# Twenty-two identity transposes at the start, and a QKV tile between two sets of transposes, in an attention and GLU kernel

## The chip, the cores and the metric

The kernel runs on one core of a Trainium2 chip. The metric is the device time of one execution in microseconds (us): 1578.9 us is the median of three runs (1578.4 to 1580.97). The engines carry the profile's names: PE (matrix multiplies and transposes; PEld is its weight load), DVE, ACT, POOL, and SP, which here only issues DMAs. Each engine works through its own instructions strictly in the order in which they were put in its queue, and waits where one of them needs something that isn't there yet.

## The reference

One transformer block over 2048 tokens of width 576, in float32:

```python
x = A_x
h = x + _A_ref(_layernorm(x), A_wqkv, A_wo)      # 32 heads of 18, window 8, dilation 2
h2 = h + _B_ref(_layernorm(h), B_w_gate, B_w_up, B_w_down)   # (sigmoid(x Wg) * (x Wu)) Wd, 4608 wide
```

In the attention a token at position s sees only positions s, s-2, ..., s-14, so its parity and its half of the sequence split the tokens into four blocks of 512.

## The kernel before

**Tiles.** The tokens are four blocks (`BLOCKS`), each of four 128-token tiles j = 0 to 3. To keep float32 precision each operand of a multiply is split in two: a "hi" part, an ACT copy with rounding (L104 and its like, in `split`), and a "lo" part, a DVE subtraction (L105). The width of 576 is 512 + 64: the four main chunks have a hi and a lo tile (`th`, `tl`), the last 64 columns are held twice in a fifth chunk of `th`, whose lower half is made lo by DVE (L109, in `split_rest`). A product (`tok_major`) is 14 matmuls over these chunks; the last two (L159, L160) use the fifth chunk.

**The opening.** `opening()` loads the tokens of block 0 and the QKV weights of head group 0 (`wr`), and does block 0's layer norm, its transposes and its first four QKV tiles. Its order on each engine is written by hand: `ch(key, fn)` queues an instruction behind the last one of the same engine in this chain. Per tile j the chain has `stats` (DVE bn_stats, POOL power), `norm` (DVE L491, L492), `tr` (PE, four main transposes L497 into a bank of the tag `mm`, one of the rest, L499, into a bank of the tag `acc`), `x_hi` (ACT L504, L505), `x_lo` (DVE L509, L511), and `heads_of` (PE, one QKV tile). The weights have `w_hi(c)` (ACT L516) and `w_lo(c)` (DVE L519) for five chunks c. Behind it, `qkv_w(1, ...)` loads and splits the weights of head group 1 (`ws`, three buffers for five chunks; hi at L104, lo at L105). On DVE its lo parts are told to come after `x_lo(1)`; its hi parts on ACT are not part of the chain.

**What sets the order elsewhere.** A list scheduler orders each engine's instructions by priority (`tc.high_priority`), by explicit "after this one" marks (`tc.issue_after`) and by its own estimate of when operands are ready. An instruction that it believes ready early can so be put ahead of another of higher priority. The order is fixed when the kernel is built.

**QKV and attention.** The rest of the first 220 us are QKV tiles on PE (16 tiles for each head group) while the attention (`attention`, in steps between `yield`s) runs on DVE from stores of q, k and v in DRAM that are loaded again by SP. Its large steps are the products L189 and L215 and the reduction L193, some 2.5 us each.

**The front.** `front()` projects block 0's attention output with `wo`, adds the residual, and does the second layer norm and its transposes. It is a generator over four `proj_j`, one for each j, in lock step: the first `next(fr)` issues the main transposes of all four tiles (L146) and their splits, the second the rest transposes (L150) and their splits, the third and fourth the two halves of the projection (L157 and on, DVE L262), later ones the norm (L123 to L128) and its transposes. Every transpose set takes a PSUM bank in turn, of the `mm` tag (three) or the `acc` tag (five, shared with the QKV tiles). The first `next(fr)` waits for L226, the end of block 0's attention; the rest transposes wait for the L428 copies as well. Before the front, `more` has issued two QKV tiles of block 2; two more, and the four of block 3, are left to fill PE between the front's steps.

**After it** the GLU products begin (`single`, L746 and L753, with DVE L766 and ACT L793), with the attention of block 1 still going on DVE. When block 1's last group is done (L226), POOL stores it (L228, L230), SP loads it again (`oj`, L707), and `proj_scr` transposes it on PE.

Of the kernel before, what the change touches and what calls it, by code (L numbers as in the profile page):

```python
# [21 lines left out]
P = 128  # L22
# [38 lines left out]
def kernel(ctx, tc, x, wqkv, wo, wmlp, out):  # L61
    nc = tc.nc
    dve, act, pool, pe, sp = nc.vector, nc.scalar, nc.gpsimd, nc.tensor, nc.sync
# [14 lines left out]
    ident = cst.tile([P, P], F32, name="ident")  # L78
# [19 lines left out]
    def f32(ap):  # L98
        return ap.bitcast(F32)
# [30 lines left out]
    def ln_stats(xj, junk):  # L130
        mv = sm.tile([P, 2], F32, bufs=4, name="mv")
        rstd = sm.tile([P, 1], F32, bufs=4, name="rstd")
        act.activation(junk[:, :D], xj, AF.Copy, scale=-1.0 / D, accum_out=mv[:, 0:1])
        sq = act.activation(junk[:, :D], xj, AF.Square, bias=mv[:, 0:1], accum_out=mv[:, 1:2])
        pool.tensor_scalar(rstd, mv[:, 1:2], 1.0 / D, EPS, ALU.mult, ALU.add)
        pool.tensor_tensor(rstd, rstd, mhalf, ALU.pow)
        pool.tensor_tensor(mv[:, 0:1], mv[:, 0:1], rstd, ALU.mult)
        return mv[:, 0:1], rstd, sq
# [98 lines left out]
    def drain(gen):  # L237
        for _ in gen:
            pass
# [54 lines left out]
    def th_tile():  # L294
        return xt.tile([P, 5, TB], F32R, tag="th", bufs=3, name="th")

    def tl_tile():
        return xt.tile([P, 4, TB], F32R, tag="tl", bufs=4, name="tl")
# [24 lines left out]
    def mm_tile():  # L323
        return psp.tile([P, 512], F32, tag="mm", bufs=3, name="mm")

    def acc_tile():
        return psp.tile([P, 512], F32, tag="acc", bufs=5, name="acc")

    def tok_tile(shape=(P, NS, DX)):
        return stk.tile(list(shape), F32, tag="tok", bufs=2, name="tok")  # L330
# [7 lines left out]
    def load_x(b, js=range(NS), t=None):  # L338
        e, hf = BLOCKS[b]
        if t is None:  # L340
            t = sah.tile([P, NS, D], F32, bufs=2, name="h")
        for j in js:
            sp.dma_start(t[:, j], xv[e, hf][:, j])
        return t
# [26 lines left out]
    def raw_w(g):  # L371
        if g == 3:
            wr = sah.tile([P, NS, D], F32, bufs=2, name="h").rearrange("p j d -> p (j d)")
            wr = wr[:, :QC].rearrange("p (c n) -> p c n", c=5)
        else:
            wr = swo.tile([P, 5, NQ], F32, tag="wo", name="wr")
        for c in range(5):
            sp.dma_start(wr[:, c], wqkv[g][:, c * NQ:(c + 1) * NQ])
        return wr
# [16 lines left out]
    def qkv(b, g, T, w):  # L396
        e, hf = BLOCKS[b]
        ev = ev_tile([P, 3, NS, CG])
        for j in range(NS):
            ps = acc_tile()  # L400
            passes.append(tok_major(ps, NQ, *T, slice(j * P, (j + 1) * P), w[:, 0], w[:, 1]))
            with tc.high_priority(HI):
                act.activation(ev[:, :, j], ps[:, :NQ].rearrange("p (t c) -> p t c", t=3), AF.Copy)
            yield
        r0 = LP + hf * TB
        with tc.high_priority(HI):
            act.dma_start(qscr[b][g], ev[:, 0].rearrange("p j c -> p (j c)"))
            for t, s in ((1, kscr), (2, vscr)):
                act.dma_start(s[e][g][r0:r0 + TB, :].rearrange("(p j) c -> p (j c)", p=P),
                              ev[:, t].rearrange("p j c -> p (j c)"))  # L410
        emitted.add((b, g))
# [46 lines left out]
    def opening():  # L458
        xb = load_x(0, (0, 1))
        wr = raw_w(0)  # L460
        load_x(0, (2, 3), xb)
        th, tl = th_tile(), tl_tile()
        xn = tok_tile()
        qw = saw.tile([P, 2, 5, NQ], F32R, tag="qw", bufs=2, name="qw")
        T.append((th, tl))
        w.append(qw)
        last = {}

        def ch(key, fn):
            with ExitStack() as way:  # L470
                way.enter_context(tc.high_priority(3 * HI))
                if key in last:
                    way.enter_context(tc.issue_after(getattr(last[key], "ins", last[key])))
                last[key] = fn()

        nr, pv, pr = {}, {}, {}

        def stats(j):
            bs = sm.tile([P, 2, 6], F32, bufs=4, name="bs")
            mv = sm.tile([P, 2], F32, bufs=4, name="mv")  # L480
            rstd = sm.tile([P, 1], F32, bufs=4, name="rstd")
            nr[j] = mv[:, 0:1], rstd
            for k in range(2):
                ch(dve, lambda: dve.bn_stats(bs[:, k], xb[:, j, k * DH2:(k + 1) * DH2]))
            ch(dve, lambda: dve.bn_aggr(mv, bs))
            ch(dve, lambda: dve.tensor_scalar(rstd, mv[:, 1:2], EPS, None, ALU.add))
            ch(pool, lambda: pool.tensor_tensor(rstd, rstd, mhalf, ALU.pow))

        def norm(j):
            m, r = nr[j]  # L490
            ch(dve, lambda: dve.tensor_scalar(xn[:, j, :D], xb[:, j], m, r, ALU.subtract, ALU.mult))  # L491
            ch(dve, lambda: dve.tensor_copy(xn[:, j, D:DX], xn[:, j, DM:D]))  # L492

        def tr(j):
            pv[j], pr[j] = mm_tile(), acc_tile()
            for c in range(4):
                ch(pe, lambda: pe.transpose(pv[j][:, c * P:(c + 1) * P],  # L497
                                            xn[:, j, c * P:(c + 1) * P], ident))
            ch(pe, lambda: pe.transpose(pr[j][:, :P], xn[:, j, DM:DX], ident))  # L499

        def x_hi(j):
            js = slice(j * P, (j + 1) * P)
            pv[j] = pv[j].rearrange("p (c n) -> p c n", c=4)
            ch(act, lambda: act.activation(th[:, 0:4, js], pv[j], AF.Copy))  # L504
            ch(act, lambda: act.activation(th[:, 4, js], pr[j][:, :P], AF.Copy))  # L505

        def x_lo(j):
            js = slice(j * P, (j + 1) * P)
            ch(dve, lambda: dve.tensor_tensor(tl[:, :, js], pv[j], f32(th[:, 0:4, js]),  # L509
                                              ALU.subtract))  # L510
            ch(dve, lambda: dve.tensor_tensor(th[64:128, 4, js], pr[j][64:128, :P],  # L511
                                              f32(th[64:128, 4, js]), ALU.subtract))
            ends.append(last[dve])

        def w_hi(c):
            ch(act, lambda: act.activation(qw[:, 0, c], wr[:, c], AF.Copy))  # L516

        def w_lo(c):
            ch(dve, lambda: dve.tensor_tensor(qw[:, 1, c], wr[:, c], f32(qw[:, 0, c]),  # L519
                                              ALU.subtract))  # L520

        call = qkv(0, 0, T[0], qw)
        ends = []

        def heads_of(j):
            ch(pe, lambda: (next(call), passes[-1])[1])

        stats(0)
        stats(1)
        norm(0)  # L530
        w_hi(0)
        tr(0)
        norm(1)
        w_hi(1)
        tr(1)
        w_lo(0)
        w_hi(2)
        w_lo(1)
        x_hi(0)
        x_lo(0)  # L540
        w_hi(3)
        w_lo(2)
        w_hi(4)
        stats(2)
        x_hi(1)
        w_lo(3)
        w_lo(4)
        heads_of(0)
        with tc.high_priority(3 * HI):
            n3, r3, sq = ln_stats(xb[:, 3], xn[:, 3])  # L550
        norm(2)
        tr(2)
        x_lo(1)
        heads_of(1)
        x_hi(2)
        ch(act, lambda: act.activation(xn[:, 3, :D], xb[:, 3], AF.Identity, bias=n3, scale=r3))
        ch(act, lambda: act.activation(xn[:, 3, D:DX], xn[:, 3, DM:D], AF.Copy))
        x_lo(2)
        tr(3)
        heads_of(2)  # L560
        x_hi(3)
        x_lo(3)
        heads_of(3)
        drain(call)
        return ends
# [75 lines left out]
    fr = front()  # L641
# [10 lines left out]
        step(ag, 1)  # L652
    last = passes[-1]
    with tc.issue_after(getattr(last, "ins", last)):
        for _ in range(2):
            next(fr)
    for b in (2, 3):
        for j, _ in enumerate(more if b == 2 else qkv(b, 3, T[b], w[3])):
            with ExitStack() as way:
                if (b, j) == (2, 0):  # L660
                    way.enter_context(tc.issue_after(getattr(passes[-1], "ins", passes[-1])))
                next(fr, END)
            step(ag, 1)
        if b == 2:
            with tc.high_priority(2 * HI):
                wg = xt.tile([P, WC], F32, tag="tl", bufs=4, name="wg0")
                sp.dma_start(wg, wmlp[0])
                ww = first_split(wg)
# [699 lines left out]
```

## Time and profile before

| | before |
|---|---|
| median of 3 runs | 1578.9 us |
| profiled execution | 1584.01 us |
| its span, first to last instruction | 1582.2 us |
| PE busy | 1551.0 us (98%) |
| DVE busy | 1255.2 us (79%) |
| ACT busy | 879.2 us (56%) |
| POOL busy | 199.9 us (13%) |
| PE idle before its first work | 6.6 us |

The profiled execution was 1.8 us longer than its span, and 5.1 us longer than the median of the runs. PE is busy nearly throughout, and DVE in most of the first third (its 40 slices of the span read 9 from the sixth to the nineteenth). Times in the views are from the span's start.

### The profile page before, as it was taken

How to read it: one execution, taken by the hardware profiler on the slowest of the kernel's cores; microseconds unless marked ns; L12 is line 12 of the kernel's file. 1: busy time of each engine (PE TensorE's matmuls, PEld its weight loads, DVE VectorE, ACT ScalarE, POOL GpSimd, SP SyncE). 2: the span in 40 equal slices, each digit the busy share in tenths (PEclk: the TensorE clock that was granted, in tenths of full speed). 3: DMA queues.
4: the chain of work that ended last, by engine and by line, in shares of the span. 5: the costliest groups of instructions: out<-in, count | busy, mean ns of one | idle time of the engine just before them, and what ended most of it. 6: DMA issues, size and time to landing. Idle time of an engine off the chain costs nothing.

```text
span 1582.2 us, 22347 instructions
## 1 busy us (share of the span) xinstructions
PE 1551.0 (98%) x8520; PEld 1377.3 (87%) x8520; DVE 1255.2 (79%) x1883; ACT 879.2 (56%) x1584; POOL 199.9 (13%) x249
## 2 busy tenths in 40 slices
PE   8999999999999999999999999999999999999998
PEld 7999888887888888888888888888888888888887
DVE  6998999969999999999426588866777776677755
ACT  6632244435555645566542355766777766777660
POOL 2300000020000010000101010112112112111210
PEclk9999999999999999999999999999999999999999
DMA  8646445365566677664683524999899989999983
GB/s 284 215 168 220 179 185 190 108 235 183 133 167 170 164 176 192 157 162 109 161 242 125 181 81 126 193 181 177 170 180 186 173 173 181 173 173 186 181 169 120
DMA packets 77147, 273.95 MB, mean 173 GB/s; under 512 B 8336, under 2 KB 14224, under 8 KB 76144
## 3 DMA queue, kind: packets, MB, share of 16 engines
q0 software_dynamic: 28192, 107.29, 37.5%
q1 hardware_dynamic: 41216, 145.11, 27.2%
q10 hardware_dynamic: 7632, 20.12, 3.3%
q8 instruction: 66, 1.08, 0.3%
q14 instruction: 41, 0.34, 0.1%
HBM read 143.98 MB, written 130.87 MB: 174 GB/s over the span
## 4 chain that ended last, share of the span: by engine, by line
PE 58%; issue 16%; DVE 11%; DMA 8%; POOL 4%; ACT 2%; SPq 0%; ACTq 0%; POOLq 0%; DVEq 0%
PE b L746 27%; PE dp L864 13%; PE dp L926 6%; PE b L753 5%; PE acc L157 4%; POOL h L935 3%; DMA wg<-in_wmlp_dram 3%; DVE pr L189 2%; DVE pr L215 1%; DVE lg L193 1%; DVE w L105 1%; DVE pr L221 1%; PE b L157 1%; PE bgp L157 1%; DMA x<-tok 1%
## 5 line engine op out<-in xcount | busy, mean ns | idle before, releaser
L746 PE MATMUL b<-tl,w 128*128 128x512 f32 x1704 | 432.6, 393 | 5.1 <-ACT s L820 3.2
L746 PEld LDWEIGHTS b<-tl,w 128*128 128x128 f32 x1704 | 307.9, 188 | 63.6 <-ACT s L820 4.7
L746 PE MATMUL b<-th,w 128*128 128x512 f32 x1344 | 346.2, 392 | 1.5 <-DVE s L839 1.5
L746 PEld LDWEIGHTS b<-th,w 128*128 128x128 f32 x1344 | 244.8, 188 | 46.5 <-DVE s L839 1.9
L932 ACT ACTIVATE ev<-dp 128x576 f32<-128x576 f32 x224 | 144.7, 646 | 63.2 <-PE dp L926 58.9
L753 PE MATMUL b<-th,w 128*128 128x512 f32 x568 | 175.7, 390 | 0.0
L104 ACT ACTIVATE w<-wg 128x384 fp32r<-128x384 f32 (+1 forms) x186 | 110.8, 601 | 111.1 <-PE b L753 48.8
L935 POOL DMA_DIRECT2D h<-ev x128 | 110.0, 860 | 458.6 <-ACT ev L932 444.7
L157 PE MATMUL acc<-qw,th 128*128 128x432 f32 x512 | 154.3, 362 | 2.5 <-DVE th L109 2.3
L105 DVE TENSOR_TENSOR w<-wg,w 128x640 fp32r<-128x640 f32 (+1 forms) x186 | 120.8, 656 | 41.3 <-ACT w L104 41.1
L105 DVE TENSOR_TENSOR w<-tw,w 128x512 fp32r<-128x512 f32 x120 | 82.6, 688 | 82.1 <-ACT w L104 81.5
L753 PEld LDWEIGHTS b<-th,w 128*128 128x128 f32 x568 | 106.5, 188 | 23.2
L864 PE MATMUL dp<-d,h1h 128*128 128x288 f32 x640 | 119.9, 297 | 0.0
L864 PE MATMUL dp<-d,h0h 128*128 128x288 f32 x608 | 114.1, 297 | 0.8 <-DVE tail L874 0.8
L872 ACT ACTIVATE stage<-dp 128x576 f32<-128x576 f32 x104 | 66.9, 645 | 70.1 <-PE dp L864 69.8
L157 PEld LDWEIGHTS acc<-qw,th 128*128 128x128 f32 x512 | 96.6, 189 | 8.4 <-DVE th L109 3.5
L864 PEld LDWEIGHTS dp<-d,h1h 128*128 128x128 f32 x640 | 99.7, 190 | 3.0
L104 ACT ACTIVATE w<-tw 128x512 fp32r<-128x512 f32 x120 | 75.4, 628 | 46.5 <-PE b L746 40.0
L864 PEld LDWEIGHTS dp<-d,h0h 128*128 128x128 f32 x608 | 95.1, 190 | 4.3 <-DVE tail L874 1.0
L157 PE MATMUL acc<-qw,tl 128*128 128x432 f32 x256 | 92.6, 362 | 0.1
L189 DVE TENSOR_TENSOR pr<-kw,q 128x2304 f32<-128x2304 f32 x32 | 81.8, 2556 | 8.8 <-DMA kw<-k 8.7
L880 POOL DMA_DIRECT2D h<-stage x26 | 31.0, 1194 | 436.3 <-ACT stage L872 350.1
(310 smaller groups left out, 2955.5 us busy)
## 6 DMA issues: line engine op xcount, KB each, us to landing
h<-ev POOLq DMA_DIRECT2D x96, 576.0 KB, 7.1
wg<-in_wmlp_dram SPq DMA_DIRECT2D x47, 928.0 KB, 5.9
h<-stage POOLq DMA_DIRECT2D x26, 1152.0 KB, 9.5
wg<-in_wmlp_dram SPq DMA_DIRECT2D x36, 640.0 KB, 4.3
kw<-k SPq DMA_DIRECT2D x16, 792.0 KB, 5.2
vw<-v SPq DMA_DIRECT2D x16, 792.0 KB, 4.3
wd<-in_wmlp_dram SPq DMA_DIRECT2D x18, 576.0 KB, 7.4
h<-ev POOLq DMA_DIRECT2D x32, 288.0 KB, 6.9
```

Of the source, the lines that this page charges most:

```text
L104: act.activation(hi, src, AF.Copy)
L105: splits.append(dve.tensor_tensor(lo, src, f32(hi), ALU.subtract))
L157: pe.matmul(ps[:, :n], a[:, c, js], m[:, c], start=k == 0, stop=False)
L189: dve.tensor_tensor(pr, both(kw, u), q[:, us].unsqueeze(2).broadcast_to([P, 2, W, CG]), ALU.mult)
L746: pe.matmul(ps, wt[:, a, k0 + c], xx[:, m + c], start=first and k == 0, stop=k == 5, skip_group_check=True)
L753: pe.matmul(ps, wt[:, a, k0], xx[:, 4], start=False, stop=a == 1, skip_group_check=True)
L864: pe.matmul(ps[:, i, :DH2], a[:, js], d[:, m, i * DH2:(i + 1) * DH2], start=k == 0, stop=k == n)
L872: act.activation(hv, ps, AF.Copy)
L880: pool.dma_start(hacc[b], hs, accum_op=ALU.add, max_dma_last_dim=8 * D)
L926: pe.matmul(ps[:, i, :DH2], a[x][:, js], m[y], start=k in (0, 1, 3) and q == 0, stop=q == 2, skip_group_check=True)
L932: act.activation(hs[:, k % 2], ps[:, :, :DH2], AF.Copy)
L935: pool.dma_start(hsev[:, u, k0:k + 1], hs[:, :k + 1 - k0], accum_op=ALU.add, max_dma_last_dim=8 * D)
```

## The change

Two edits. In the opening, ahead of all other work on PE, 22 transposes of the identity into a bank of the tag `mm` that nobody reads. And in the front, the second `next(fr)`, which issues the rest transposes, moves from before the third QKV tile of block 2 to behind it.

```diff
         nr, pv, pr = {}, {}, {}
+        pre = mm_tile()
+        for _ in range(22):
+            ch(pe, lambda: pe.transpose(pre[:, :P], ident, ident))
...
     last = passes[-1]
     with tc.issue_after(getattr(last, "ins", last)):
-        for _ in range(2):
-            next(fr)
+        next(fr)
     for b in (2, 3):
         for j, _ in enumerate(more if b == 2 else qkv(b, 3, T[b], w[3])):
             with ExitStack() as way:
                 if (b, j) == (2, 0):
                     way.enter_context(tc.issue_after(getattr(passes[-1], "ins", passes[-1])))
+                    next(fr)
                 next(fr, END)
             step(ag, 1)
```

In the changed file the lines of the opening and the front stand three lower than before (L504 is L507, L516 is L519); L104, L105, L109, L146, L150, L157, L189, L193 and L262 keep their numbers. The diff alone doesn't show that the scheduler, which counts the 22 transposes as time in which ACT is free, puts other instructions elsewhere.

ACT in the opening, before. The rows are the engine, line, operation, output<-inputs, shape and count; `qw<-wr` is head group 0's weights, `qw<-ws` head group 1's, `th<-mm` and `th<-acc` the hi parts of the tokens:

```order
L516 ACTIVATE qw<-wr 128x432 x3
L504 ACTIVATE th<-mm 128x4x128
L505 ACTIVATE th<-acc 128x128
L516 ACTIVATE qw<-wr 128x432 x2
L504 ACTIVATE th<-mm 128x4x128
L505 ACTIVATE th<-acc 128x128
L104 ACTIVATE qw<-ws 128x432 x2
L133 ACTIVATE tok,mv<-h 128x576
L104 ACTIVATE qw<-ws 128x432
```

and with the change:

```order
L519 ACTIVATE qw<-wr 128x432 x3
L104 ACTIVATE qw<-ws 128x432 x3
L507 ACTIVATE th<-mm 128x4x128
L508 ACTIVATE th<-acc 128x128
L519 ACTIVATE qw<-wr 128x432 x2
L507 ACTIVATE th<-mm 128x4x128
L508 ACTIVATE th<-acc 128x128
L133 ACTIVATE tok,mv<-h 128x576
```

Three weight chunks of head group 1, each of which waits for its own load, now stand ahead of the hi parts of block 0's first tile. DVE's order in the opening is the same in both.

DVE in the front, before, from the reduction of block 1's attention that runs when the transposes are done (`tl<-...` are lo parts of the main chunks, `th<-...` of the rest, `pr<-kw,q` the attention's product, `h<-h,mm` the first projected tile):

```order
L193 TENSOR_REDUCE lg<-pr 128x128
L105 TENSOR_TENSOR tl<-mm,th 128x4x128
L109 TENSOR_TENSOR th<-acc,th 64x128 x3
L109 TENSOR_TENSOR th<-mm,th 64x128
L105 TENSOR_TENSOR tl<-mm,th 128x4x128
L105 TENSOR_TENSOR tl<-acc,th 128x4x128 x2
L189 TENSOR_TENSOR pr<-kw,q 128x2304
L262 TENSOR_TENSOR h<-h,mm 128x288
```

and with the change:

```order
L193 TENSOR_REDUCE lg<-pr 128x128
L105 TENSOR_TENSOR tl<-mm,th 128x4x128 x2
L105 TENSOR_TENSOR tl<-acc,th 128x4x128 x2
L189 TENSOR_TENSOR pr<-kw,q 128x2304
L109 TENSOR_TENSOR th<-acc,th 64x128 x3
L109 TENSOR_TENSOR th<-mm,th 64x128
L262 TENSOR_TENSOR h<-h,mm 128x288
```

The four rest parts moved from ahead of the attention's product to behind it.

PE at the same place, before (`acc<-qw,th` opens the QKV tile):

```order
L146 MATMUL mm<-ident,tok 128x128 x5
L150 MATMUL mm<-ident,tok 128x128
L146 MATMUL mm<-ident,tok 128x128 x3
L146 MATMUL acc<-ident,tok 128x128 x5
L150 MATMUL acc<-ident,tok 128x128 x3
L146 MATMUL acc<-ident,tok 128x128 x3
L157 MATMUL acc<-qw,th 128x432
```

and with the change:

```order
L146 MATMUL mm<-ident,tok 128x128 x8
L146 MATMUL acc<-ident,tok 128x128 x8
L157 MATMUL acc<-qw,th 128x432
...
L160 MATMUL acc<-qw,th 128x432
L150 MATMUL acc<-ident,tok 128x128 x3
L150 MATMUL mm<-ident,tok 128x128
```

The sixteen main transposes now come in one run, then the whole QKV tile, then the four rest transposes; before, the QKV tile came last. From there to about L864's first products DVE, ACT and PE also take the projection's tail and the norms in another order (the first two tiles' norms earlier, the last two later); behind that the three engines' orders are the same again.

## The prediction

> **What bounds the kernel now.** I read the page's first lines, then who waited for whom on PE over the whole span, then on PE between 13 and 179 us alone, then the chain of waits, and last the timelines of the two places that the change touches. The page:
>
> ```profile
> span 1582.2 us, 22347 instructions
> PE 1551.0 (98%) x8520; PEld 1377.3 (87%) x8520; DVE 1255.2 (79%) x1883; ACT 879.2 (56%) x1584; POOL 199.9 (13%) x249
> ```
>
> PE's waits over the span (line, releaser: us in total, times, longest), and after the "..." those between 13 and 179 us, where there is one:
>
> ```profile
> PE mm L497 <- DVE tok L491: 6.6, 1, 6.6
> PE b L146 <- DMA oj<-o: 4.2, 1, 4.2
> PE acc L157 <- DVE th L109: 2.3, 2, 1.6
> ...
> PE acc L157 <- DVE th L109: 0.6, 1, 0.6
> ```
>
> So PE has almost no slack from the opening to 179 us: what delays its start there arrives whole at 179 us. The change touches the time after the 6.6 us, and two stalls in the front, the 1.6 us above and one of 1.7 us. Whether these are worth anything is told by the chain of waits (start, us, what), here around 119 and 308 us:
>
> ```profile
> 119.17 0.54 ACT ev L403
> ...
> 128.47 2.57 DVE pr L189
> ...
> 307.86 0.68 DVE kw L226
> ...
> 309.46 6.85 DMA o<-kw
> ```
>
> ```profile
> 319.42 1.11 PE L146 MATMUL b<-ident,oj 128*128 128x128 f32 x4 [4.23 <-DMA oj<-o]
> ```
>
> Up to 119.17 the chain is PE; there the last q, k, v of a head group leave, DVE waits for them until 128.47, and from then to 308.54 it is the attention on DVE that counts. Its last result is stored and loaded, and PE stands for 4.23 us until 319.42. **Two consequences.** A delay of PE in the opening goes through 119 us into DVE's chain and out at 319 us. And PE time saved in the front, at 180 to 190 us, is not saved at 319 us: it makes the 4.23 us longer, unless DVE's own chain gets shorter there.
>
> **The opening: ACT's order.** Before, ACT, DVE, SP and PE did this (start, us, what), with the landing of the third `ws` load in the last line (us from its issue):
>
> ```profile
> 7.75 0.60 ACT L504 ACTIVATE th<-mm 128x512 fp32r<-128x512 f32 x1 [0.50 <-PE mm L497]
> 8.40 1.02 ACT L516 ACTIVATE qw<-wr 128x432 fp32r<-128x432 f32 x2
> 8.74 0.69 DVE L509 TENSOR_TENSOR tl<-mm,th 128x512 fp32r<-128x512 f32 x1
> 11.66 0.55 ACT L104 ACTIVATE qw<-ws 128x432 fp32r<-128x432 f32 x1
> 12.66 0.46 PE L160 MATMUL acc<-qw,th 128*128 128x432 f32 x1
> 4.98 1.41 SPq L386 DMA_DIRECT2D ws<-in_wqkv_dram x3
> ws<-in_wqkv_dram SPq DMA_DIRECT2D x1, 216.0 KB, 5.2
> ```
>
> The three loads of `ws` are issued at 4.98, about 5.47 and about 5.96 us (three in 1.41 us). The third lands at 5.96 + 5.2 = 11.16 us; that it was there at 11.66, when ACT used it, bounds it from above. SP's order up to them does not change, so they land then again. With the change ACT must take all three before L504 of tile 0. Two copies in a row start 1.02 - 0.56 = 0.46 us apart, so L504 starts at 11.16 + 0.46 = 11.62 instead of 7.75: 3.87 us late. DVE's L509 needs its result: 11.62 + 0.60 = 12.22, say 12.25, instead of 8.74, **3.5 us late**. From there the chain of waits before was DVE without a gap, to the third tile's transposes on PE:
>
> ```profile
> 8.83 0.60 DVE tl L509
> ...
> 12.61 0.52 DVE tok L491
> 13.17 0.66 PE mm L497 x4
> ```
>
> DVE's order there is the same, and its other inputs come in time (the last two weight copies on ACT end near 13.3 us, DVE needs them at 15). So 13.17 becomes 16.7: +3.5 us. Bounds: 3.4, against the 8.83 us of the chain, and 3.9, all of ACT's delay.
>
> **The 22 transposes.** They wait only for the identity, which POOL finishes at 1.44 us. Their price is bounded by the first real ones:
>
> ```profile
> 1.16 0.28 POOL masks.py:199 TENSOR_SCALAR_AFFINE_SELECT ident<-ident 128x128 f32<-128x128 f32 x1
> 6.59 1.12 PE L497 MATMUL mm<-ident,tok 128*128 128x128 f32 x4 [6.59 <-DVE tok L491]
> 8.64 0.71 PE L157 MATMUL acc<-qw,th 128*128 128x432 f32 x1
> 10.64 0.36 PE L157 MATMUL acc<-qw,tl 128*128 128x432 f32 x1
> 16.80 0.60 PE L497 MATMUL mm<-ident,tok 128*128 128x128 f32 x4
> ```
>
> Four cost 1.12 us at the start and 0.60 us later, so 22 cost between 3.3 and 6.2 us and end between 4.8 and 7.7 us. The first real transpose is due at 6.59, so they could push it by up to 1.1 us; ACT's new wait until 11.62 covers that, so I cost them at nothing (without that cover: 1.1 us at most). What they could gain is covered as well: real transposes 0.5 us sooner feed L504, which waits for `ws`. Even in the old order DVE was at L519 until 8.83, so L509 could not have started sooner.
>
> **The clock in the new gap.** PE has its second tile's transposes done soon after the second norm, near 8.1 us, and then nothing until 12.22: 4.1 us. The nearest row is the stall of 4.23 us before 319.42. The granted clock there (stretch, length, busy times of PE, PEld, DVE, ACT and POOL, then the clock, DMA share and GB/s):
>
> ```profile
> 317.00:319.00 2.00, 0.00 (x0) 0.00 (x0) 0.00 (x0) 0.00 (x0) 0.00 (x0) 0.68 0.78 204
> 319.00:320.00 1.00, 0.58 (x3) 0.58 (x4) 0.00 (x0) 0.00 (x0) 0.00 (x0) 0.50 1.03 410
> 324.00:325.00 1.00, 1.00 (x6) 0.83 (x6) 0.56 (x1) 0.60 (x1) 0.00 (x0) 0.72 0.97 401
> ```
>
> It fell to 0.50 before PE resumed and came back near 324.5, some 5 us after; in the opening the step from 0.71 to 0.36 us came 4.0 us after the first transpose (6.59 to 10.6). I take the gap of 4.1 us to do the same. Then the first QKV tile runs at half clock: its second matmul waits for L509 (12.25 + 0.69 = 12.94), and twelve more steps lead to its last one. A step at full clock is 0.20 us (12 in 2.35 us in the row below), at half clock 0.39 (below it, the weight load's waits for lo parts):
>
> ```profile
> 20.24 2.35 PE acc L157 x12
> PEld acc L157 <- DVE tl L509: 0.8, 2, 0.6
> ```
>
> With the clock back 4.0 us after 12.22, eight steps are slow and four fast: 12.94 + 3.1 + 0.8 = 16.9, against 12.66 + 3.5 = 16.2 at which DVE would let it run: +0.7 us. Bounds: 0 if the clock holds, +1.4 if all twelve are slow (17.6). The other of PE's two waits for a lo part, 0.8 - 0.6 = 0.2 us in the second tile, goes, since DVE is ahead then: I take **+0.5 us**, and 4.0 us for the opening.
>
> The Trainium skill speaks on this gap: in "TensorE: Matmul & The Clock Gate", Part 1, the gate is fed by a free-running window of about 3.4 us, and an idle one throttles. By that rule as an estimate, a gap of 4.1 us holds a whole window in about one phase of five, the term would be 0.1 and the opening 3.6 us. The 4.23 us stall fell, as the rule allows it to. The same page (Part 4) says that transposes don't count as activity; the rows above disagree, since the clock rose 2.0 us after the first projection matmul (8.64) but 4.0 us after the first transpose; by the page the third rival below would have no gain from the clock.
>
> **The front.** Before, on PE and DVE:
>
> ```profile
> 181.79 0.33 PE L150 MATMUL mm<-ident,tok 128*128 128x128 f32 x1 [1.70 <-DVE tok L428]
> 185.30 0.46 PE L157 MATMUL acc<-qw,th 128*128 128x432 f32 x1 [1.65 <-DVE th L109]
> 188.14 0.29 PE L157 MATMUL mm<-wo,th 128*128 128x288 f32 x1
> 184.23 0.69 DVE L105 TENSOR_TENSOR tl<-mm,th 128x512 fp32r<-128x512 f32 x1
> 184.95 0.71 DVE L109 TENSOR_TENSOR th<-acc,th 64x128 fp32r<-64x128 f32 x3
> 187.70 2.55 DVE L189 TENSOR_TENSOR pr<-kw,q 128x2304 f32<-128x2304 f32 x1
> 190.20 0.45 DVE L262 TENSOR_TENSOR h<-h,mm 128x288 f32<-128x288 f32 x1
> ```
>
> (In these old times; 4 us are to be added.) Both PE stalls go: sixteen main transposes from 179.4 to 181.3, the QKV tile to 183.9, the rest transposes to 184.4, and PE is at the projection some 3.7 us sooner than 188.14. But its last two matmuls need the fifth chunk, and DVE now makes it (L109) behind the attention's product: four L105 from 184.23 at about 0.65 us, L189 from 186.8 to 189.3, the first L109 at 189.6. So **the stalls are not removed but gathered** into one of about 3 us in the first projected tile (from 186.4 to 189.6), which then ends near 190.0; before, its 14 matmuls from 188.14 ended just ahead of L262 at 190.20. DVE does the same work to L262: 190.4 for 190.20. Between 178 and 308.5 us DVE is busy for 124.5 of 130.5 us in the old order (first row: stretch, length, DVE busy, clock, DMA share, GB/s), so 6.0 us are idle; the largest single wait is in the second row:
>
> ```profile
> 178.00:308.50 130.50, 124.51 (x177) 1.00 0.45 164
> 227.15 0.69 DVE L766 TENSOR_TENSOR s<-s,b 128x512 f32<-128x512 f32 x1 [1.25 <-PE b L753]
> ```
>
> Following the new order by these durations, DVE waits some 1.5 us for later tiles of the projection (it takes the norms one tile after another now), and gets back 1.1 of the 1.25 us at L766, which it reaches later: **+0.4 us** by 250 us. Bounds: -1.5 if the wait at L766 goes, a quarter of a microsecond more elsewhere, and none comes, +2 if all new ones stay.
>
> **Sum.** 3.5 + 0.5 + 0.4 = +4.4 us: a span of 1586.6 after 1582.2. The profiled execution with its 1.8 us outside the span stood 5.1 us over the median; I take the same distance again, so the median goes from 1578.9 to 1583.3. Nothing is added behind 319 us, where the orders are the same.
>
> **The rivals.** Differences under 0.2%, 3.2 us here, are about what a measurement of this kernel can't tell from none.
> - *Forecast*: ACT stands at `ws`, and it comes out at 319 us: +3.3 to +6. Chance 0.57.
> - *Mostly absorbed*: the clock holds in the gap (0 for 0.5) and the front gives back the 1.5 us of its bound: 3.5 + 0 - 1.5 = +2.0, 1580.9 us. For it: DVE has 6.0 us idle to give. Against it: its largest single wait is 1.25 us, and the new order brings waits of its own. Chance 0.27.
> - *As the edits read*: the clock is up, the stalls of 1.70 and 1.65 us go, and ACT does not stand. Then -3.35 us and more, 1575.5 us. It decides if the first L504 still starts near 7.7. For it: all that PE saves would be real if PE alone set the end. Against it: the `ws` rows, and the 4.23 us in which PE waits anyway. Chance 0.08.
> - *More than forecast*: the gap is cold throughout (+1.4) and the front's waits all stay (+2): 3.5 + 1.4 + 2 = +6.9, 1585.8 us, and more if the late norms make PE wait for its first GLU operands. Chance 0.08.
>
> So faster 0.08, same 0.27, slower 0.65. The likeliest case's own range is 1582.2 to 1585; with the absorbed case below and the worse one above, 1579.5 to 1587.
>
> **What would show it.** In the changed profile: ACT's first `th<-mm` copy near 11.6 us, with a wait for the `ws` load ahead of it; 22 transposes done by about 6.5 us; the third tile's transposes on PE at 17 us; granted clock or matmul durations at half in the first QKV tile; no PE wait for L428, but one of about 3 us for L109 in the first `mm<-wo` tile; block 1's last L226 near 313 us and PE's resumption near 324. I am wrong if the first `th<-mm` copy starts before 10 us, if the 3.5 us are there but the store of block 1's attention is less than 2 us late, or if the time before 319 us moves less than that behind it.

## The result, and the profile after

| | before | changed |
|---|---|---|
| median, first comparison (5 runs each) | 1580.97 us | 1587.24 us |
| median, second comparison (35 and 12 runs) | 1581.0 us | 1588.67 us |
| profiled execution's span | 1582.2 us | 1585.6 us |
| mean granted clock of it | 0.996 | 0.993 |

The change makes the kernel slower: ratio 1.0038, 95% interval 1.0026 to 1.005, and again 1.0038 (1.002 to 1.0055) in the second comparison. By medians that is +6.3 and +7.7 us, where +4.4 was forecast. The page of the changed kernel:

```profile
span 1585.6 us, 22385 instructions
PE 1556.2 (98%) x8542; PEld 1383.3 (87%) x8542; DVE 1256.1 (79%) x1883; ACT 880.7 (56%) x1584; POOL 198.9 (13%) x249
```

PE is 5.2 us busier with only 22 transposes more, which take 4 us; DVE and ACT do the same work in 0.9 and 1.5 us more.

**The opening.** PE, ACT and DVE in the changed kernel (start, us, engine, line, operation, then in brackets the idle time before it and what ended it):

```profile
1.50 4.00 PE L479 MATMUL mm<-ident 128*128 128x128 f32 x22 [1.50 <-POOL ident masks.py:199]
6.67 0.66 PE L500 MATMUL mm<-ident,tok 128*128 128x128 f32 x4 [1.17 <-DVE tok L494]
10.49 1.72 ACT L104 ACTIVATE qw<-ws 128x432 fp32r<-128x432 f32 x3 [3.28 <-DMA ws<-in_wqkv_dram]
12.11 0.58 ACT L507 ACTIVATE th<-mm 128x512 fp32r<-128x512 f32 x1
12.75 0.73 PE L157 MATMUL acc<-qw,th 128*128 128x432 f32 x1 [4.28 <-ACT th L507]
17.96 0.40 PE L160 MATMUL acc<-qw,th 128*128 128x432 f32 x1
130.34 2.56 DVE L189 TENSOR_TENSOR pr<-kw,q 128x2304 f32<-128x2304 f32 x1 [4.36 <-DMA kw<-k]
```

The 22 transposes end at 5.5 us. ACT stands at the `ws` copies, L507 starts at 12.11, PE waits 4.28 us, and the last matmul of the first QKV tile starts 5.3 us later than before (12.66). At the attention's product that followed the last q, k, v store (128.47 before), only 1.87 us of that are left. The clock there (stretch, length, busy times of PE, PEld, DVE, ACT and POOL, then the granted clock, DMA share and GB/s):

```profile
11.00:12.00 1.00, 0.00 (x0) 0.00 (x0) 0.00 (x0) 0.97 (x3) 0.00 (x0) 0.60 1.05 408
12.00:18.00 6.00, 5.25 (x14) 4.47 (x15) 5.08 (x12) 3.94 (x11) 1.99 (x4) 0.50 0.35 114
18.00:19.00 1.00, 1.00 (x9) 0.93 (x8) 0.94 (x3) 0.61 (x2) 0.00 (x0) 0.99 1.00 330
```

It fell inside the gap and stayed at half for the whole first tile.

**The front.** PE's sixteen main transposes, the end of the QKV tile, and the projection, in the changed kernel:

```profile
182.32 1.03 PE L146 MATMUL mm<-ident,tok 128*128 128x128 f32 x8
186.62 0.36 PE L160 MATMUL acc<-qw,th 128*128 128x432 f32 x1
187.55 0.33 PE L150 MATMUL acc<-ident,tok 128*128 128x128 f32 x1 [0.36 <-DVE tl L105]
187.75 0.38 PE L157 MATMUL mm<-wo,th 128*128 128x288 f32 x1
190.94 0.40 PE L159 MATMUL mm<-wo,th 128*128 128x288 f32 x1 [0.18 <-DVE th L109]
```

Both old stalls are gone and only 0.36 and 0.18 us stand in their place: PE ran nine matmuls of the second projected tile ahead of the first tile's last two, so there was work while DVE made the fifth chunk. PE is at the projection at 187.75, where it was at 188.14 before, although it came to the main transposes 2.9 us later (182.32; 179.39 before). Forty microseconds on, the loss is there. First the rows of DVE and SP in the kernel before, then those of DVE, SP, ACT and PE now:

```profile
214.30 2.55 DVE L215 TENSOR_TENSOR pr<-vw,lg 128x2304 f32<-128x2304 f32 x1
217.29 20.66 SPq L702 DMA_DIRECT2D wg<-in_wmlp_dram  x3
```

```profile
220.77 2.56 DVE L215 TENSOR_TENSOR pr<-vw,lg 128x2304 f32<-128x2304 f32 x1
223.35 0.32 SPq L178 DMA_DIRECT2D vw<-v  x1
223.76 17.88 SPq L705 DMA_DIRECT2D wg<-in_wmlp_dram  x3
234.88 0.74 ACT L104 ACTIVATE w<-wg 128x640 fp32r<-128x640 f32 x1 [4.73 <-DMA wg<-in_wmlp_dram]
235.52 0.58 ACT L796 ACTIVATE s<-b 128x512 f32<-128x512 f32 x1
236.16 0.96 PE L749 MATMUL b<-tl,w 128*128 128x512 f32 x2 [2.40 <-ACT s L796]
```

With the rest splits moved, norms and weight splits come ahead of DVE's second L215, which starts 6.5 us later. SP's load of `vw` needs the buffer that this L215 frees, and issues when it ends (220.77 + 2.56 = 223.33). The GLU weights `wg` stand behind it in SP's queue, though they need nothing of it: 223.76 instead of 217.29. ACT waits 4.73 us for them, L796 stands behind that copy, and PE waits for L796. A second stall follows for `h0h`, near 283 us. PE's waits over the span, all of over 2 us (the last two rows are the front's, the first is the opening's):

```profile
PE acc L157 <- ACT th L507: 4.3, 1, 4.3
PE b L749 <- ACT s L823: 3.4, 3, 1.7
PE b L146 <- DMA oj<-o: 2.9, 1, 2.9
PE b L146 <- DVE tl L105: 2.9, 1, 2.9
PE dp L867 <- ACT h0h L104: 2.6, 1, 2.6
PE b L749 <- ACT s L796: 2.4, 1, 2.4
```

Block 1's last L226 and PE's resumption behind it:

```profile
315.11 0.75 DVE L226 TENSOR_TENSOR kw<-kw 128x576 f32<-128x576 f32 x1
325.41 0.90 PE L146 MATMUL b<-ident,oj 128*128 128x128 f32 x3 [2.89 <-DMA oj<-o]
```

L226 is 7.3 us later than 307.78 before, PE's resumption 6.0 us later than 319.42: the store and load of `oj` happened to be quicker than the 4.23 us wait of the old profile. In all profiles but one that follow, this wait is 2.7 to 3.3 us; the old profile was a slow one there. The 7.3 us are those of one execution: in a second profile of the changed kernel (e8 below, the fastest of its twelve executions) L226 was at 308.84, 1.1 us later than before. There the stall for L796 was 2.46 us again, but that for `h0h` only 0.4 us.

### The profile page after: what moved, and what is told of

The parts are those of the page before. It is cut to its first block, busy times and chain, and to the rows that moved or that the text cites. A ratio compares the mean times of both kernels' runs of the same rounds, so it can differ in the third digit from the quotient of the medians.

```text
span 1585.6 us, 22385 instructions
## 1 busy us (share of the span) xinstructions
PE 1556.2 (98%) x8542; PEld 1383.3 (87%) x8542; DVE 1256.1 (79%) x1883; ACT 880.7 (56%) x1584; POOL 198.9 (13%) x249
## 4 chain that ended last, share of the span: by engine, by line
PE 47%; issue 28%; DVE 9%; POOL 7%; DMA 6%; ACT 2%; SPq 0%; POOLq 0%; ACTq 0%; DVEq 0%
PE b L749 19%; PE dp L867 13%; POOL h L938 7%; PE acc L157 6%; DMA wg<-in_wmlp_dram 4%; PE b L756 3%; DVE pr L189 1%; DVE pr L215 1%; DVE lg L193 1%; DVE w L105 1%; PE b L157 1%; PE bgp L157 1%; DVE pr L221 1%; DVE s L769 1%; DMA tail<-h 1%
## 5 line engine op out<-in xcount | busy, mean ns | idle before, releaser
L104 ACT ACTIVATE w<-wg 128x384 fp32r<-128x384 f32 (+1 forms) x186 | 111.0, 601 | 114.8 <-PE b L756 51.6
L157 PE MATMUL acc<-qw,th 128*128 128x432 f32 x512 | 155.2, 364 | 4.3 <-ACT th L507 4.3
L105 DVE TENSOR_TENSOR w<-wg,w 128x640 fp32r<-128x640 f32 (+1 forms) x186 | 120.8, 655 | 42.3 <-ACT w L104 41.8
L105 DVE TENSOR_TENSOR w<-tw,w 128x512 fp32r<-128x512 f32 x120 | 82.4, 687 | 83.0 <-ACT w L104 82.3
L157 PEld LDWEIGHTS acc<-qw,th 128*128 128x128 f32 x512 | 97.2, 190 | 9.0 <-ACT th L507 4.5
L104 ACT ACTIVATE w<-tw 128x512 fp32r<-128x512 f32 x120 | 75.4, 628 | 45.7 <-PE b L749 40.1
L157 PE MATMUL acc<-qw,tl 128*128 128x432 f32 x256 | 93.0, 363 | 0.0
L189 DVE TENSOR_TENSOR pr<-kw,q 128x2304 f32<-128x2304 f32 x32 | 81.7, 2552 | 6.1 <-DMA kw<-k 6.0
```

The lines of the kernel that those rows point to most:

```text
L104: act.activation(hi, src, AF.Copy)
L105: splits.append(dve.tensor_tensor(lo, src, f32(hi), ALU.subtract))
L157: pe.matmul(ps[:, :n], a[:, c, js], m[:, c], start=k == 0, stop=False)
L189: dve.tensor_tensor(pr, both(kw, u), q[:, us].unsqueeze(2).broadcast_to([P, 2, W, CG]), ALU.mult)
```

## The experiments

Twelve kernels, 12 executions each, beside 35 of the kernel before in each of three comparisons. The comparisons were on three chips, so kernels of different comparisons are set against each other by their distance from their own kernel before. Medians, and the ratio to before with its 95% interval:

| run | edit | median, us | before, us | ratio |
|---|---|---|---|---|
| e1_tr22 | the 22 transposes alone | 1585.13 | 1581.38 | 1.0023 (1.0006 to 1.004) |
| e2_front | the moved step alone | 1584.82 | 1581.38 | 1.0026 (1.0009 to 1.0043) |
| e3_tr22_act | e1, ACT's old order | 1581.67 | 1581.38 | 1.001 (0.9989 to 1.003) |
| e4_act_alone | ACT's new order, no transposes | 1586.85 | 1581.38 | 1.0038 (1.002 to 1.0055) |
| e5_front_vw | e2, one load on POOL | 1579.23 | 1581.0 | 0.9988 (0.9974 to 1.0002) |
| e6_vw | before, the same load on POOL | 1582.32 | 1581.0 | 1.0002 (0.9987 to 1.0017) |
| e7_all | the change, both mends | 1584.53 | 1581.0 | 1.0019 (1.0005 to 1.0033) |
| e8_again | the changed kernel | 1588.67 | 1581.0 | 1.0038 (1.002 to 1.0055) |
| e9_fill | e1, 12 more transposes in the gap | 1581.68 | 1581.66 | 1.0 (0.9985 to 1.0014) |
| e10_change_vw | the change, the load on POOL | 1582.56 | 1581.66 | 1.0009 (0.9998 to 1.0021) |
| e11_tr22_act | e3 once more | 1582.15 | 1581.66 | 1.0006 (0.9991 to 1.0021) |
| e12_front_vw | e5 once more | 1580.95 | 1581.66 | 0.9996 (0.9983 to 1.0009) |

### The two halves of the change

e1 is the kernel before with the first part of the diff, e2 with the second.

> The 22 transposes of the identity alone, the rest transposes left where they were. ORDER theory (the cost of the opening comes from the three L104 copies that stand ahead of the first L507 on ACT): the opening as in the changed kernel, first L507 near 12.1 us, a wait of PE of about 4.3 us for it, half clock from about 11.5 to 18 us, PE +5.3 us at the first QKV tile, +2.9 us at 119 us, about +1.5 us on DVE at 180 us; time +1 to +3 us against before. FRONT theory (the whole loss of the change lies in the front, what the opening loses is absorbed by the DVE-bound stretch ahead of 190 us): same opening, time within 0.5 us of before. TRANSPOSE theory (the transposes cost by themselves, as PE work) gives the same as ORDER here and is told apart in the next but one.

> The moved rest transposes alone, the opening left as it was. QUEUE theory (the moved step saves PE 2 to 3 us by the last QKV tile, but norms and splits come ahead of DVE's second L215 at 214 us, the load of vw on SP's queue waits for it, and the wg loads stand behind that load): second L215 5 us later than before, vw and wg loads 5 us later on SP, a wait of 2 to 2.5 us for ACT's s in the first GLU tiles and one of about 2.5 us for h0h near 280; PE 3 to 5 us behind at 300 us, time +2 to +5 us. OPENING theory (the loss of the change comes from the opening): time -2 to 0 us, no later wg loads.

Measured: +3.75 us, above the +1 to +3 written ahead, and +3.4 us. The sum, 7.2 us, is about what the whole change cost (6.3 and 7.7). Each half has its own loss. In e1 PE's wait for L507 was 4.10 us. In e2 the second L215 started at 220.63, and this came of it:

```profile
223.21 0.32 SPq L178 DMA_DIRECT2D vw<-v  x1
223.62 18.09 SPq L702 DMA_DIRECT2D wg<-in_wmlp_dram  x3
236.23 0.73 PE L746 MATMUL b<-tl,w 128*128 128x512 f32 x2 [2.61 <-ACT s L793]
```

So the queue's part needs nothing of the opening. The FRONT and OPENING theories, which put all of the loss into one half, are out.

### ACT's order in the opening

e3 holds the `qw<-ws` copies of head group 1 behind the second tile's copies on ACT too, where before only DVE's lo parts were held:

```diff
-            ends.append(last[dve])
+            ends.append((last[dve], last[act]))
...
-                    way.enter_context(tc.issue_after(getattr(after, "ins", after)))
+                    for i in after:
+                        way.enter_context(tc.issue_after(getattr(i, "ins", i)))
```

> The 22 transposes, with the L104 copies of the second qw held behind the second tile's last copy on ACT, so that ACT, DVE and POOL run in the order of before. ORDER theory: first L507-like copy back near 7.8 us, PE's wait for it back to about 0.6 us, the ten real transposes at 0.66 us or less instead of 1.12, the first QKV tile ends at 12.2 to 12.7 us; time -1 to +0.3 us against before. TRANSPOSE theory: the loss of the first of these runs stays, +1 to +3 us.

e4 has no transposes; its opening issues the three copies itself, ahead of `x_hi(0)`:

```diff
         w_lo(1)
+        qw1 = saw.tile([P, 2, 5, NQ], F32R, tag="qw", bufs=2, name="qw")
+        for c in range(3):
+            ws = sas.tile([P, NQ], F32, tag="wst", bufs=3, name="ws")
+            sp.dma_start(ws, wqkv[1][:, c * NQ:(c + 1) * NQ])
+            ch(act, lambda: act.activation(qw1[:, 0, c], ws, AF.Copy))
         x_hi(0)
```

> No transposes of the identity; the three L104 copies of the second qw put ahead of the first L504 on ACT by hand, as they stand in the changed kernel. ORDER theory: first L504 at 11.6 to 12.1 us, a wait of PE of about 3.5 to 4.5 us, half clock in the first tile, PE +2.9 us at 119 us; time +1 to +3 us, as with the 22 transposes alone. TRANSPOSE theory: the copies fit beside the cold PE, time within 0.5 us of before.

The first `th<-mm` copy of e3, and PE behind it; then e4:

```profile
7.41 0.60 ACT L508 ACTIVATE th<-mm 128x512 fp32r<-128x512 f32 x1
8.27 0.44 PE L157 MATMUL acc<-qw,th 128*128 128x432 f32 x1
54.10 0.47 PE L157 MATMUL acc<-qw,th 128*128 128x432 f32 x1 [1.46 <-ACT ev L404]
```

```profile
12.05 0.58 ACT L508 ACTIVATE th<-mm 128x512 fp32r<-128x512 f32 x1
12.69 0.73 PE L157 MATMUL acc<-qw,th 128*128 128x432 f32 x1 [3.59 <-ACT th L508]
187.93 0.47 PE L150 MATMUL mm<-ident,tok 128*128 128x128 f32 x1 [2.44 <-DVE tok L432]
```

e3's opening is the old one, and by medians most of the 3.75 us is gone: +0.3 us, and +0.5 in its repeat below. By the intervals (-1.7 to +4.7 us for e3, +0.9 to +6.3 for e1) the two can't be told apart. e4 makes the gap without a single transpose. So ACT's order makes the 4 us stall, not PE's added work. What the stall costs in time can't be read from e4's +5.5 us, which is above the +1 to +3 written ahead: the order of DVE moved too, and a stall of 2.44 us came up at 188 us.

> The 22 transposes with the L104 copies held behind the second tile's copies, once more. ORDER theory: -1 to +1 us. TRANSPOSE theory (the transposes cost by themselves, as the 2.9 us wait near 840 us that only kernels with them show would have it, with a spell at half clock behind it): +1 to +3 us.

The repeat's +0.5 us lies in ORDER's range, but its interval (-1.4 to +3.3 us) reaches over all of TRANSPOSE's; neither it nor e3 can be told from before. Their profiles show where a mended opening still loses: PE of e3 was 0.1 us behind before up to 50 us and 2.0 us from 80 us on, where e1's 5.05 us had shrunk to 3.3. The 22 transposes change SP's order as well, and the attention's first loads come later (before, then e3):

```profile
27.86 0.34 SPq L176 DMA_DIRECT2D q<-q  x1
```

```profile
29.91 0.38 SPq L176 DMA_DIRECT2D q<-q  x1
```

The attention's exponential, which stands ahead of the QKV copies in ACT's queue, then comes 2.1 us later (51.13; 49.03 before), and the wait of 1.46 us at 54 us follows: 1.47 us in the repeat and 1.36 in e7. It is not the transposes' alone: e2, with SP's old order, loaded `q` at 29.76 and had 1.43. What makes the load late is not shown.

### The queue in front of the GLU weights

e5 is e2 with one load on another queue:

```diff
-            sp.dma_start(vw.rearrange("p j c -> p (j c)"), window(vscr[e][g], hf))
+            (pool if (b, g) == (1, 2) else sp).dma_start(vw.rearrange("p j c -> p (j c)"), window(vscr[e][g], hf))
```

> The moved rest transposes alone, and the load of vw of block 1's third group issued from POOL instead of SP, so that the first two wg loads no longer stand behind it. QUEUE theory: the wg loads issue at or before 217 us again, no wait of 2.6 us for ACT's s near 236 and no half clock behind it; PE about 0.5 us or less behind before at 245 us instead of 4.1; the later wait for h0h near 282 smaller or gone; time 2 to 4 us under the moved step alone (1584.8), that is -1 to +2 us against before. DVE theory (the norms and splits that come ahead of DVE's L215 delay the attention, and that alone decides): last L226 still near 313 us, time as with the moved step alone, +3 to +4 us.

> Control: the kernel before with the same one load issued from POOL. Both theories: the wg loads had no late consumer in the kernel before (DVE and ACT take them without a wait of PE), so within 1 us of before; any gain here is to be taken off what the run ahead shows.

> The moved step with the load of vw on POOL, once more: QUEUE theory -2.5 to -0.5 us against before, the fastest of all; if the first result was chance, -0.5 to +1 us.

SP and PE in e5, and POOL, which now waits for L215 at no cost:

```profile
215.39 21.40 SPq L702 DMA_DIRECT2D wg<-in_wmlp_dram  x2
220.86 0.61 POOL L178 DMA_DIRECT2D vw<-v  x1 [11.44 <-DVE pr L215]
233.03 1.20 PE L746 MATMUL b<-tl,w 128*128 128x512 f32 x4 [1.33 <-DVE w L105]
```

DVE's order is still e2's, with L215 at 217.99 and thus late against the loads, but the loads no longer are: in the place of the stall of 2.61 us is one of 1.33 us for a weight part, that for `h0h` fell from 2.20 to 0.60, and last L226 came at 306.19 instead of 313.35. Time: -1.8 us where e2 has +3.4, each against its own kernel before. That is 5.2 us less, more than the 2 to 4 written ahead, and the control e6 shows no gain of its own. QUEUE stands, and the DVE theory falls. The repeat was again under before, by 0.7 us. Both intervals reach past 1: against before it is no difference that could be told; against the changed kernel it is 9.4 us in one comparison (1588.67 - 1579.23).

### Together, and the clock

e7 has both mends; e10 the second alone; e8 is the changed kernel itself.

> All of the change, with both mends: the L104 copies held behind the second tile's copies on ACT, and the load of vw from POOL. ORDER and QUEUE theories together: no wait of 4.3 us in the opening, no wait near 236 us, time -2 to +2 us against before, 5 to 7 us under the changed kernel. If the transposes or the moved step cost by themselves: +2 us or more.

> The changed kernel once more, beside the three others on one chip: +5 to +7.5 us if the losses of its two parts (+3.75 and +3.4 us by medians) add up, with a mean granted clock 0.001 to 0.003 under that of before; +3.5 to +4.5 us if they share one loss.

> The changed kernel with the load of vw on POOL alone; the order on ACT in the opening is left as the change has it. ORDER and QUEUE theories: the front's loss goes, the opening's +3.8 us stays on top of what the moved step alone gave with this mend (-1.6 us by means): +1.5 to +3.5 us against before, 4 to 6 us under the changed kernel. If the kernel with both mends (+2.9 us by means) is no faster than this one, the order on ACT costs nothing there and the 22 transposes cost by themselves.

e8 repeated the loss, just above the +5 to +7.5 us written ahead. e10 came down to +0.9 us, 6.8 us less than e8, as the queue's part should and more than the 4 to 6 written ahead. But e7 came out at +3.5 us where -2 to +2 was expected, no better than e10 (the intervals overlap): the mend of ACT's order was worth nothing here. By what was written ahead this speaks for a price of the 22 transposes themselves, against e3 and e11.

Six kernels have the transposes without the front's loss, and together they say more than each alone. By means, against the same kernel without transposes, those with ACT's new order and its stall lost 3.9 us (e1), 2.7 (e10 less e12) and 0.2 (e9, below); those with ACT's old order lost 1.6 (e3), 0.1 (e11) and 4.5 (e7 less e5). The two groups average 2.3 and 2.1 us, each give or take some 1.1. So the transposes cost about 2 us under either order of ACT, and a price of the order on top of that is not shown. This grouping was made after the results were known.

A price that comes with the transposes is in the profiles: near 836 us PE waits for an L105 that waits on a `wg` load (e3, then e12):

```profile
841.04 0.47 PE L146 MATMUL b<-ident,oj 128*128 128x128 f32 x1 [2.91 <-DVE tl L105]
```

```profile
831.41 0.44 PE L146 MATMUL b<-ident,oj 128*128 128x128 f32 x2 [1.80 <-DVE tl L105]
```

In all eight profiles with the transposes this wait is 2.7 to 3.0 us, in all six without them 1.8 to 2.0, though between before and e3 DVE, ACT and POOL have one order throughout, and SP's differs only before 35 us. The `wg` load itself takes longer. Here are the queue that carries instructions and the load, between the load's issue and its landing, in e3 and then in before, where that queue has no row (packets, MB, share of the DMA engines; then KB and us from issue to landing):

```profile
q8 instruction: 1, 0.02, 0.5%
wg<-in_wmlp_dram SPq DMA_DIRECT2D x1, 928.0 KB, 10.4
```

```profile
wg<-in_wmlp_dram SPq DMA_DIRECT2D x1, 928.0 KB, 9.5
```

In all eight profiles with the transposes one such packet, of 16 KB and 0.9 us, starts 5.8 to 8.4 us after the load's issue, and the load takes 10.2 to 10.5 us. In all six without them the packet comes only 2.6 to 3.1 us after the landing, and the load takes 9.3 to 9.5. A whole profile has 66 or 67 of these packets for some 17040 matmuls and weight loads of PE, one for about 256, so they are probably PE's own instructions, and 22 more transposes move them. No run moves the packet alone, so this is the likely cause and not a shown one. A spell at half clock came with this wait in all eight and in three of the six. From these profiles an estimate of the price is 1 us for the wait and 1 us for the clock, about what the six kernels lost.

e9 is e1 with 12 more transposes behind `tr(1)`, to shorten the gap; every other engine keeps e1's order.

> The 22 transposes alone as in the first run, and 12 more of them behind the second tile's transposes, so that PE stands idle for some 2 us instead of 4.1 ahead of the first QKV matmul; the order on ACT, DVE, POOL and SP is that of the first run, so the first L507 stays near 12 us. CLOCK theory (4 us of idle PE lowers the clock, and that is a part of the opening's loss): no half clock between 12 and 18 us, first QKV tile done in 5 us less 2.3, PE about +2.5 us against before at 15 us instead of +5.1, and +0 to +0.7 us at 185 us instead of +1.7; time 1 to 3 us under the first run's +3.8. ORDER theory without the clock: PE still +5 us, time as the first run.

PE and the granted clock in e9:

```profile
8.38 1.47 PE L540 MATMUL mm<-ident 128*128 128x128 f32 x12
13.17 0.47 PE L157 MATMUL acc<-qw,th 128*128 128x432 f32 x1 [3.32 <-ACT th L507]
```

```profile
14.00:15.00 1.00, 1.00 (x6) 0.95 (x7) 0.97 (x3) 1.00 (x4) 0.00 (x0) 1.00 0.08 20
16.00:18.00 2.00, 2.00 (x7) 1.53 (x6) 1.94 (x5) 0.41 (x2) 1.80 (x3) 0.50 0.00 0
```

They ran at 0.12 us each, not 0.18, and L507 came half a microsecond later, so the gap was 3.32 us and not 2. The clock still fell, but two us after PE resumed, and for 3.4 us instead of e1's 6.8. PE's first tile ended 4.8 us late (2.5 expected), and at 100 us PE was 2.9 us late where e1's was 3.3. The time is level with before, 3.7 us less than e1: the direction that CLOCK wants, but what CLOCK said of the profile did not come, so it is not shown. And a PE that leaves the opening 3 us late need not make the kernel slower.

## Why the prediction was right in sign, and where its steps failed

The forecast of +4.4 us had the sign and, with +6.3 and +7.7 measured, two thirds of the size. Both differences lie between the +0.6 and +8.1 us that the stated range of 1579.5 to 1587 leaves around 1578.9; the median of 1587.24 itself is just above it, as the kernel before came out at 1580.97 in that comparison. That the size came near is in part luck: the term that made most of the sum is not shown to cost anything, and two that were put at little or nothing made up for it.

- **ACT stands at `ws` (3.5 us).** The stall came as described. L507 started at 12.11, not 11.62, as the copies ended later, and L512 at 12.73 instead of 12.25. Its price did not show: the transposes lost 2.3 us with this stall and 2.1 without it.
- **The clock in the gap (0.5 us).** Mis-sized in this execution. The third tile's transposes came at 18.19 where 17 was predicted: the first tile ran at half clock from end to end, the upper bound that the prediction gave (+1.4). A PE that was brought up by 22 transposes and then stood had to come up again: 0.50 until 18 us. In e8 the spell was half as long, and the first tile's last matmul started at 16.78, the 4.0 us after 12.66 that were predicted and 0.1 more. The estimate worked out from the Trainium skill's window ("TensorE: Matmul & The Clock Gate", Part 1), that a gap of 4.1 us throttles in one phase of five, is not what the runs show: of the eight stalls of 3.6 us and more all eight throttled.
- **"What delays its start there arrives whole at 179 us".** Wrong. PE was 4.7 us late up to 50 us and 2.9 from 80 us to 179, and of these 1.87 were left on DVE at 130. Between 50 and 80 us PE's weight load had waited 1.6 us for L109 before, and did not now; the prediction had looked at the 0.6 us of PE itself. By one of its own signs the rest of the path, out at 319 us, is not borne out either: block 1's last L226 was 7.3 us late in the first profile, but 1.1 us in e8 and 1.1 in e1 (308.90). So that the opening's total of 4.0 met e1's +3.75 is luck as far as the runs show. e1's mean granted clock was lower, 0.9949 against 0.9968 over its 12 and 35 executions. A straight line through all 249 executions, with an offset for each kernel, gives 1.35 us for 0.001 of clock, so 2.6 of the 3.75 us go with the clock; what lowered it in e1 and not in e9 is open.
- **The 22 transposes at nothing.** Right on PE in the opening: they were done at 5.5 us and the first real ones cost 0.66 us instead of 1.12. Wrong for the kernel: the six kernels put them at some 2 us, and the longer wait near 836 us comes with them. That transposes bring the clock up, as argued against Part 4 of the Trainium skill's page "TensorE: Matmul & The Clock Gate", is borne out by that 0.66 us.
- **The front: "the stalls are not removed but gathered" (+0.4 us).** This is the step that failed most, by some 3 us. The gathered stall never came. PE was ahead, as a bare reading of the edit says. What was not followed is the new order past DVE into SP's queue: from L215 to `vw`'s buffer, to the `wg` loads behind `vw`, to ACT, to PE. The sentence on "late norms" that make PE wait for GLU operands, in the fourth rival, named the victim but not the path; e2 measured +3.4, and e5 took it away by moving one load.
- **"Nothing is added behind 319 us".** Not borne out: the orders are the same there, but the wait near 836 us is 1 us longer in all eight profiles with the transposes.

The rival that the edits do what they read as was out in the changed kernel. Once the loads are free, its front part shows on PE: at the old places e5 waits only 1.2 us, for L105. In time it can't be told: the two results are 1.8 and 0.7 us under before, with intervals that reach past 1.

## What to carry to other kernels

When an edit reorders one engine, follow every buffer that the moved instructions free into the DMA queue that waits for it, and look at what stands behind that DMA: a load that needs nothing can be the one that is late. Harmless extra work at the head of a list-scheduled kernel moves the scheduler's idea of time, and with it the order of engines that the edit never names; pin those orders, or read them all. A stall that an edit makes early can be gone before the end, so follow it through every later wait, those of the weight load too, before it is priced. Price a stall of PE of 2 us and more at its length plus the clock: 33 of 43 here brought a spell at half clock, which cost 1.7 or 3.4 us.

## What the runs showed of the hardware

Every spell at less than full clock, in all fourteen profiles up to 1550 us, was 3.4 or 6.8 us at half, and so lost 1.7 or 3.4 us: 29 of the one and 9 of the other. The Trainium skill's window of about 3.4 us ("TensorE: Matmul & The Clock Gate", Part 1) agrees with that. Its condition, an idle window, does not: stalls much shorter than a window often brought a spell. Counting each stall of PE behind its first work, without the start of e4, and as behind it each spell that began between the stall's start and 2 us after its end:

| length of the stall | spell behind it |
|---|---|
| 3.6 us and more | 8 of 8 |
| 2.6 to 3.4 us | 19 of 22 |
| 2.0 to 2.6 us | 6 of 13 |
| 1.8 to 2.0 us | 4 of 9 |
| 1.0 to 1.8 us | 0 of 31 |

One spell of the 38 came without a stall of 1 us, in e7's opening behind a wait of 0.90 us. Stalls of one length go either way. The `oj` wait was 3.02 us in e2 and 3.00 in e1; the clock right behind it, in e2 and then in e1:

```profile
324.00:328.00 4.00, 3.89 (x29) 3.29 (x28) 2.62 (x4) 1.91 (x4) 0.00 (x0) 1.00 1.06 406
```

```profile
320.00:321.00 1.00, 1.00 (x6) 1.00 (x6) 0.00 (x0) 0.54 (x1) 0.00 (x0) 0.50 0.96 321
```

Such spells go with about half of the scatter between executions of one kernel (the straight line above takes 53% of their variance): before ran from 1575.0 to 1588.06 us in one comparison, and its profile had 10.2 us at half clock where e12's had 3.4 and the changed kernel's 20.4. A single pair of profiles can't place 3 us here; the twelve executions could. And one start was cheaper cold. PE of e4 had done ten transposes before its stall of 3.59 us; its matmuls took 0.73 us at first and 0.35 from 16.66 us on, and the clock on record shows nothing of it:

```profile
12.00:16.00 4.00, 3.31 (x8) 2.70 (x9) 3.20 (x9) 3.89 (x11) 0.43 (x1) 1.00 0.43 154
```

PE of e1, brought up by 22 transposes and let go, stayed at half until close to 19 us; its first tile ended 5.2 us late, e4's 4.6. So a granted clock of 1.00 at the start of a profile does not say that PE is at full speed; the matmuls' own durations do.
